# Pooled attention and a token/channel mixer on one core: the first batch's transposed u made by matmuls, and the fourth batch's loads gated on the second batch's transposed u

## The chip, the cores and the metric

The kernel runs on one core of a Trainium2 chip. The metric is device time in microseconds (us) of one launch. Three runs of the kernel before gave 288.86, 289.02 and 290.66 us; their median is 289.02. One further execution was profiled: it took 290.2 us, of which the profile's span covers 288.5.

## The reference

Eight batches of 576 positions, eight heads of 64 columns. Keys and values are averaged over groups of eight positions, so that each head attends over 72 pooled positions. The result x (576 x 512 per batch) goes through a mixer over positions (tokens) and one over columns (channels):

```python
k_p = k.reshape(B, H, Sp, pool, D).mean(axis=3)          # Sp = 72, pool = 8
v_p = v.reshape(B, H, Sp, pool, D).mean(axis=3)
attn = softmax(scale * np.matmul(q, k_p.transpose(0, 1, 3, 2)))
x = np.matmul(attn, v_p)  ->  (B, 576, 512)
xt = x.transpose(0, 2, 1)
h = np.maximum(xt @ w_tok1, 0.0) @ w_tok2                # 576 -> 256 -> 576 over positions
u = x + h.transpose(0, 2, 1)
h2 = np.maximum(u @ w_ch1, 0.0) @ w_ch2                  # 512 -> 1536 -> 512 over columns
out = u + h2
```

## The kernel before, in words

All operands of matmuls are bf16, sums are fp32 in PSUM; the loads cast from fp32. Batches are numbered 0 to 7, so the fourth batch of the title is batch 3 and the second is batch 1. A batch has 512 "main" positions in four blocks of 128 (j = 0 to 3) and a "tail" of 64; the tails of two batches share one tile of 128 rows. The pairs are (0, 7), (1, 2), (3, 4) and (5, 6).

A batch passes through these steps, by their names in the code:

- `pool_k` (L255 to L281): pools the keys by matmuls (L267, L271) and copies them into a block tile `kbd`, of which there are three. `pool_v` does it for the values of batches 0 and 1 on PE; from batch 2 on `sum_v` (L292) adds the values up on POOL, twelve instructions a batch.
- `do_qT` (PE) or `qT_dma` (a transposing DMA on SP, L540, from batch 2 on): the queries, transposed. Half of the positions are unit a (`jj` = 0), half unit c; the tail is unit t.
- `do_S` scores on PE, maximum and subtraction on DVE (L329, L331); `do_E` the exponential on ACT (L339); `do_PT` transposes the probabilities (PE and a copy on ACT or DVE for batches 0 and 1, L350 and L352; DMA on SP from batch 2 on, L346); `do_AV` weighs the values (L387, in batch 0 L375) and divides on DVE.
- `do_AT` / `do_both_AT`: first token matrix and Relu, into `AT`; `do_u`: second token matrix and the residual, into `um`; `do_uT`: u transposed into `uTm`, on PE for batch 0 (L530), by DMA from batch 1 on (L526).
- `channel_mix`: `do_GT` is the first channel matrix with Relu on ACT (L756, L758; L787 for the first three blocks of batch 0), `out_pieces` the second one (L771) with the residual u added on DVE (L775) and the store on SP (L803).

The order on every engine is written out by hand: lists of steps with a weight, which `weave` (L29) merges. While the channel mix of batch b runs, `second_stream` (for batch 1) or `value_stream` of batch b+1 and `score_stream` of batch b+2 are woven in. Each engine executes its instructions in that order, and one that waits holds up all that follow it on its engine. POOL issues all loads, in order, among its own additions; SP issues the transposing DMAs and the stores.

A load goes into a tile that an earlier batch has used: two sets for keys and queries, one for values (`vs`). The loads of batches 0, 1 and 2, and batch 3's keys and queries, are issued at once, as far as their tiles are free (L823 to L827, with `sum_v(2)` behind them); batch 3's values and its sums stand in `second_stream` (L670). From batch 4 on `load_gated` (L737) issues a batch's loads: a one-column copy on POOL that reads a given tile holds back all that follows on POOL, then come the loads, then `sum_v`. Batch 4's loads wait in this way for the last transposed probabilities of batch 2 (L726).

PSUM has six buffers of one bank for general use (`pa`) and two for transposes (`pt`).

Of the kernel before, what the change touches and what calls it, by code (L numbers as in the profile page):

```python
# [8 lines left out]
FP32 = mybir.dt.float32  # L9
# [39 lines left out]
def kernel(  # L49
# [10 lines left out]
):  # L60

# [240 lines left out]
    class Unit:  # L302
# [40 lines left out]
        def do_PT(self, e):  # L343
            self.pT[e] = pt_pool.tile([P, H, P], BF16, name="pT")
            if not self.by_pe:
                nc.sync.dma_start_transpose(out=self.pT[e], in_=self.probs[:, e].rearrange("p h n -> p (h n)"))  # L346
                return
            pT_ps = ps_tr.tile([SP, H, P], BF16, name="pt")
            for h in range(H):
                nc.tensor.transpose(out=pT_ps[:, h, :], in_=self.probs[:, e, h, 0:SP], identity=ident)  # L350
            by_dve = e == 0 and self.jj == 1 if self.first else e == 1
            (nc.vector.tensor_copy if by_dve else nc.scalar.copy)(out=self.pT[e][0:SP], in_=pT_ps)  # L352
# [106 lines left out]
    def token_mix(b):  # L459
# [26 lines left out]
        def do_both_AT(js, tail, last):  # L486

            fresh = not at_both
            if fresh:
                at_both.extend(ps.tile([P, DM], FP32, name="pa") for _ in range(2))  # L490
            for i, j in enumerate(js):
                for m in range(2):
                    nc.tensor.matmul(out=at_both[m], lhsT=w1m[:, j, m * P:(m + 1) * P], rhs=x_main[b][:, j, :],
                                     start=(fresh and i == 0), stop=(last and i == len(js) - 1))
            if tail:
                for m in range(2):
                    nc.tensor.matmul(out=at_both[m], lhsT=w1t[s][:, m * P:(m + 1) * P], rhs=x_tail[g],
                                     start=False, stop=False)
            if last:
                for m in range(2):  # L500
                    acts(m, at_both[m])

        def do_u(j):
            u_ps = ps.tile([P, DM], FP32, name="pa")
            by_act = b == 0 and j % 2 == 1
            if j < NJ:
                if by_act:
                    nc.tensor.matmul(out=u_ps, lhsT=ident, rhs=x_main[b][:, j, :], start=True, stop=False)
                for m in range(2):
                    nc.tensor.matmul(out=u_ps, lhsT=w2m[:, m, j, :], rhs=ATs[b][:, m, :],  # L510
                                     start=(m == 0 and not by_act), stop=(m == 1))
                if by_act:
                    nc.scalar.copy(out=u_main[b][:, j, :], in_=u_ps)
                else:
                    nc.vector.tensor_tensor(out=u_main[b][:, j, :], in0=u_ps, in1=x_main[b][:, j, :], op=ALU.add)  # L515
            else:
                for i in range(4):
                    nc.tensor.matmul(out=u_ps, lhsT=w2t[i // 2][:, i % 2, :], rhs=ATs[groups[g][i // 2]][:, i % 2, :],  # L518
                                     start=(i == 0), stop=(i == 3))
                nc.vector.tensor_tensor(out=u_tail[g], in0=u_ps, in1=x_tail[g], op=ALU.add)  # L520

        def do_uT(j):
            us = u_main[b][:, j, :] if j < NJ else u_tail[g]
            if b > 0:
                dst = uT_main[b][:, :, j * P:(j + 1) * P] if j < NJ else uT_tail[g]
                nc.sync.dma_start_transpose(out=dst, in_=us)  # L526
                return
            uT_ps = ps_tr.tile([P, 4, P], BF16, name="pt")
            for kk in range(4):
                nc.tensor.transpose(out=uT_ps[:, kk, :], in_=us[:, kk * P:(kk + 1) * P], identity=ident)  # L530
            copy = nc.scalar.copy if j % 2 else nc.vector.tensor_copy
            copy(out=uT_main[b][:, :, j * P:(j + 1) * P], in_=uT_ps)

        return do_AT, do_both_AT, do_u, do_uT
# [32 lines left out]
    def mix_stream(st, b, pooled=()):  # L567
# [3 lines left out]
        u_main[b] = u_pool.tile([P, NJ, DM], BF16, name="um")  # L571
# [4 lines left out]
        do_AT, do_both_AT, do_u, do_uT = token_mix(b)  # L576
        if b == 0:
            return do_both_AT, do_u, do_uT
# [5 lines left out]
        for j in range(nj + 1):  # L584
            if j < nj:
                add(690, do_u, j)
            if j >= 1:
                add(0 if b else 224, do_uT, j - 1)

    def first_stream():  # L590
# [5 lines left out]
        do_both_AT, do_u, do_uT = mix_stream(st, b)  # L596
# [20 lines left out]
        add(SC, t.do_S)  # L617
        add(PT, a.do_PT, 1)
        add(0, c.do_E, 2)
        add(AV, a.do_AV, 0)  # L620
        add(0, t.do_E)
        add(PT, c.do_PT, 0)
        add(AV, a.do_AV, 1)
        add(PT, c.do_PT, 1)
        add(PT, t.do_PT)
        add(1080, do_both_AT, (0, 1), False, False)
        add(AV, c.do_AV, 0)
        add(AV, t.do_AV)
        add(AV, c.do_AV, 1)
        add(1080, do_both_AT, (2,), True, False)  # L630
        add(540, do_both_AT, (3,), False, True)
        k1 = []
        add(690, do_u, 0)
        add(690, do_u, 1)
        add(224, do_uT, 0)
        add(690, do_u, 2)
        add(224, do_uT, 1)
        add(690, do_u, 3)
        add(KP, lambda: k1.append(pool_k_sum(1)))
        add(224, do_uT, 2)  # L640
        add(224, do_uT, 3)
        add(0, lambda: pool_k_copy(1, k1[0]))
        return st

    def second_stream(st):
# [7 lines left out]
        add(VP, pool_v, b)  # L653
        add(SC, a.do_S, 1)
# [9 lines left out]
        add(PT, a.do_PT, 1)  # L664
        add(SC, t.do_S)
        add(0, c.do_E, 1)
        add(AV, a.do_AV, 0)
        add(SC, c.do_S, 2)
        add(0, t.do_E)
        add(0, load, 3, (2,))  # L670
        add(0, sum_v, 3)
        add(AV, a.do_AV, 1)
        add(0, c.do_E, 2)
        add(PT, t.do_PT)
        add(PT, c.do_PT, 0)
        add(AV, t.do_AV)
        add(PT, c.do_PT, 1)
# [4 lines left out]
        mix_stream(st, b, owned(2))  # L682

# [59 lines left out]
    def channel_mix(uTs, us, dst, width, early=0):  # L743

        GT = gt_pool.tile([P, NM, width], BF16, name=f"GT{width}")
# [13 lines left out]
        def out_pieces(j, halves=1):  # L761
            n, w = NM // 3, DM // halves
            pieces = []
            for c in range(halves):
                cols, hold = slice(c * w, (c + 1) * w), {}

                def do_out(part, cols=cols, hold=hold):
                    if part == 0:
                        hold["ps"] = ps.tile([P, w], FP32, name="pa")
                    for kk in range(part * n, (part + 1) * n):  # L770
                        nc.tensor.matmul(out=hold["ps"], lhsT=GT[:, kk, j * P:(j + 1) * P], rhs=wc2[:, kk, cols],  # L771
                                         start=(kk == 0), stop=(kk == NM - 1))
                    if part == 2:
                        o_sb = out_pool.tile([P, w], FP32, name="o")
                        nc.vector.tensor_tensor(out=o_sb, in0=hold["ps"], in1=us(j)[:, cols], op=ALU.add)  # L775
                        dst(j, cols, o_sb)
# [5 lines left out]
        def do_early(m, hold, t0, t1):  # L782
            def f():
                if t0 == 0:
                    hold[m] = ps.tile([P, width], FP32, name="pa")
                for kk in range(4):
                    nc.tensor.matmul(out=hold[m][:, t0:t1], lhsT=wc1[:, kk, m * P:(m + 1) * P], rhs=uTs[:, kk, t0:t1],  # L787
                                     start=(kk == 0), stop=(kk == 3))
                if t1 == width:
# [4 lines left out]
        wide = [(432, do_early(m, hold, *t)) for t in ((0, width // 2), (width // 2, width)) for m in range(early)]  # L794
        return wide + [(864, do_GT(m0)) for m0 in range(early, NM, per)], out_pieces

    def c_stream(b):
# [11 lines left out]
        wide, chunk = channel_mix(uT_main[b], lambda j: u_main[b][:, j, :], dst_main, MAIN, 0 if b else 3)  # L809
# [15 lines left out]
    load(2)  # L825
    load(3, (0, 1))
    sum_v(2)  # L827
# [44 lines left out]
```

## Time and profile before

| | |
|---|---|
| three runs, us | 288.86, 289.02, 290.66 (median 289.02) |
| the profiled execution, us | 290.2, span 288.5 |
| busy, us (share of the span) | PE 271.0 (94%), DVE 162.4 (56%), ACT 121.3 (42%), POOL 101.5 (35%) |
| PE busy, 60 to 70 us and 70 to 80 us | 7.36 and 8.46 of 10 |
| granted PE clock, 70 to 80 us | 0.83 (1.00 in the other stretches of ten) |
| PE busy, 120 to 270 us | 148.9 of 150 |
| chain that ended last | PE 82%, DMA 7%, DVE 6%, ACT 3% |

Rows of the profile name a line of the kernel, an engine, an operation with its output and input tiles, and a count; times are us from the span's start, and a bracket holds the idle time ahead of the row and what ended it. PE's matmuls are pipelined: a row's duration runs to a modelled end, and what one matmul costs in a row of many is the distance between starts. "To landing" of a DMA counts from its issue.

### The profile page before, as it was taken

The page shows a single profiled execution, that of the slowest core. Times are in us where ns is not written, and L with a number is a line of the kernel's source. Part 1 is how long each engine was busy: PE and PEld are TensorE (multiplying, and loading weights), DVE is VectorE, ACT ScalarE, POOL GpSimd, SP SyncE. Part 2 cuts the span into 40 slices and gives each one's busy share as a digit, 9 for nine tenths or more (in the row PEclk, how much of TensorE's full clock was granted, in tenths as well). Part 3 has the DMA queues.
Part 4 walks back from the last instruction along what each step waited for, and adds up shares of the span by engine and source line. Part 5 has one row for each costly group of instructions (what it writes and reads, how often), then busy time and mean ns, then how long its engine had stood idle before and what let it go on. Part 6 is the DMA issues. An engine that isn't in the chain of part 4 may idle for free.

```text
span 288.5 us, 5632 instructions
## 1 busy us (share of the span) xinstructions
PE 271.0 (94%) x2210; PEld 147.1 (51%) x2246; DVE 162.4 (56%) x371; ACT 121.3 (42%) x222; POOL 101.5 (35%) x147
## 2 busy tenths in 40 slices
PE   6888998885999999999999999999999999999995
PEld 4554755442445554446545554465445444464463
DVE  4676268687356985386647953684558642530012
ACT  8572887113442355114553365035442561026320
POOL 8666634292780836129508423570000000000000
PEclk9999999999899999999999999999999999999999
DMA  7999999999959999998999799959524820241013
GB/s 84 185 205 198 196 204 192 174 203 146 252 88 169 166 214 195 182 183 166 172 185 155 170 218 153 157 165 162 115 54 97 194 58 36 93 109 39 27 45 110
DMA packets 102714, 42.68 MB, mean 148 GB/s; under 512 B 72480, under 2 KB 98080, under 8 KB 102688
## 3 DMA queue, kind: packets, MB, share of 16 engines
q0 software_dynamic: 36688, 17.93, 47.2%
q1 hardware_dynamic: 65856, 24.26, 43.7%
q8 instruction: 17, 0.28, 0.4%
q10 hardware_dynamic: 144, 0.13, 0.1%
q14 instruction: 9, 0.07, 0.1%
HBM read 35.85 MB, written 9.44 MB: 157 GB/s over the span
## 4 chain that ended last, share of the span: by engine, by line
PE 82%; DMA 7%; DVE 6%; ACT 3%; issue 1%; DVEq 0%
PE pa L756 31%; PE pa L771 28%; DMA qT<-qm 4%; PE pa L510 4%; PE pa L472 4%; PE pa L387 3%; DMA uTm<-um 3%; PE pa L253 2%; PE pa L326 2%; DVE sh L331 2%; DVE mx L329 1%; PE pa L267 1%; ACT prob_m L339 1%; PE pa L518 1%; ACT pT L352 1%
## 5 line engine op out<-in xcount | busy, mean ns | idle before, releaser
L771 PE MATMUL pa<-wc,GT 128*128 128x512 bf16 (+1 forms) x429 | 102.7, 373 | 1.0 <-DVE sh L331 0.2
L756 PE MATMUL pa<-uTm,wc 128*128 128x512 bf16 x357 | 90.1, 384 | 3.8 <-DMA uTm<-um 3.1
L758 ACT ACTIVATE GT<-pa 128x512 bf16<-128x512 f32 x105 | 62.5, 597 | 66.5 <-PE pa L756 62.4
L756 PEld LDWEIGHTS <-wc 128*128 128x128 bf16 x564 | 45.4, 98 | 40.6 <-DVE o L775 3.6
L771 PEld LDWEIGHTS <-GT 128*128 128x128 bf16 x444 | 41.5, 98 | 40.4
L339 ACT ACTIVATE prob_m<-sh 128x432 bf16<-128x432 f32 (+1 forms) x48 | 24.7, 522 | 60.9 <-DVE sh L331 51.1
L298 POOL TENSOR_TENSOR s<-vs 72x512 f32<-72x512 bf16 x24 | 27.6, 1148 | 49.7 <-DMA vs<-in_v_dram 48.2
L775 DVE TENSOR_TENSOR o<-pa,um 128x512 f32<-128x512 f32 (+1 forms) x33 | 22.1, 670 | 25.3 <-PE pa L771 25.3
L329 DVE TENSOR_REDUCE mx<-pa 128x6 f32<-128x432 f32 (+1 forms) x48 | 26.4, 550 | 7.6 <-PE pa L326 7.5
L331 DVE TENSOR_TENSOR sh<-pa,mx 128x432 f32<-128x432 f32 (+1 forms) x48 | 26.8, 558 | 5.1 <-DVE mx L329 0.5
L391 DVE RECIPROCAL den<-pa 128x4 f32<-128x4 f32 (+1 forms) x66 | 11.6, 176 | 24.5 <-PE pa L387 24.4
L515 DVE TENSOR_TENSOR um<-pa,xm 128x512 bf16<-128x512 f32 x30 | 20.2, 687 | 8.6 <-PE pa L510 8.6
L392 DVE TENSOR_TENSOR xm<-pa,den 128x256 bf16<-128x256 f32 x56 | 23.8, 424 | 1.9
L510 PE MATMUL pa<-AT,w2m 128*128 128x512 bf16 x64 | 18.3, 379 | 0.5 <-ACT AT L466 0.5
L299 POOL TENSOR_TENSOR s<-s 72x256 f32<-72x256 f32 x24 | 17.3, 722 | 1.9
L468 DVE TENSOR_SCALAR AT<-pa 128x512 bf16<-128x512 f32 x8 | 5.5, 692 | 21.8 <-PE pa L476 21.1
L387 PEld LDWEIGHTS <-pT 72*128 72x128 bf16 (+1 forms) x280 | 12.4, 100 | 8.8 <-issue 1.7
L326 PE MATMUL pa<-kbd,qT 128*128 128x144 bf16 x128 | 15.5, 226 | 1.4 <-DMA qT<-qm 0.9
L326 PEld LDWEIGHTS <-qT 128*128 128x128 bf16 x128 | 10.7, 98 | 10.5 <-DMA qT<-qm 1.4
L387 PE MATMUL pa<-vpx,pT 72*128 72x65 bf16 (+1 forms) x280 | 14.1, 194 | 1.1 <-DVE pT L352 0.5
L472 PE MATMUL pa<-xm,w1m 128*128 128x512 bf16 x54 | 14.4, 379 | 0.4 <-DVE xm L392 0.2
L253 PE MATMUL pa<-idle 128*128 128x288 bf16 (+2 forms) x40 | 9.8, 379 | 2.3 <-DVE pool_t L178 2.2
(122 smaller groups left out, 232.8 us busy)
## 6 DMA issues: line engine op xcount, KB each, us to landing
out_dram<-o SPq DMA_DIRECT2D x31, 256.0 KB, 2.6
km<-in_k_dram POOLq DMA_DIRECT2D x8, 512.0 KB, 7.7
qm<-in_q_dram POOLq DMA_DIRECT2D x7, 512.0 KB, 12.7
vs<-in_v_dram POOLq DMA_DIRECT2D x6, 576.0 KB, 10.1
wc<-in_moe_w_ch_dram POOLq DMA_DIRECT2D x6, 512.0 KB, 12.4
out_dram<-o SPq DMA_DIRECT2D x9, 128.0 KB, 2.4
vs<-in_v_dram POOLq DMA_DIRECT2D x2, 512.0 KB, 9.9
kt<-in_k_dram POOLq DMA_DIRECT2D x8, 64.0 KB, 7.7
```

Of the source, the lines that this page charges most:

```text
L298: nc.gpsimd.tensor_tensor(out=s4, in0=vs[:, hs, 0:4], in1=vs[:, hs, 4:8], op=add)
L326: nc.tensor.matmul(out=sc[:, (h - h0) * 2:(h - h0) * 2 + 2, :], lhsT=qTs[self.b][:, 2 * h + self.jj, :], rhs=kbd[self.b % NB][:, h], start ...
L329: nc.vector.tensor_reduce(out=mx[:, 0:n], in_=sc, axis=AX.X, op=ALU.max)
L331: nc.vector.tensor_tensor(out=sh[:, 0:n], in0=sc, in1=mx[:, 0:n, None].broadcast_to([P, n, SP]), op=ALU.subtract)
L339: nc.scalar.activation(out=self.probs[:, :, h0:h1, 0:SP].rearrange("p e h n -> p h e n"), in_=self.sh[i][:, 0:(h1 - h0) * 2].rearrange("p ...
L387: nc.tensor.matmul(out=ao[r, hh, :], lhsT=probs_of(h, r), rhs=vpx[b % NB][:, h, :], start=True, stop=True)
L392: nc.vector.tensor_tensor(out=xo[rows, hf * HP * D:(hf + 1) * HP * D].rearrange("p (h d) -> p h d", d=D), in0=ao[rows, :, 0:D], in1=den[ro ...
L472: nc.tensor.matmul(out=at_ps, lhsT=w1m[:, j, m * P:(m + 1) * P], rhs=x_main[b][:, j, :], start=(j == 0), stop=False)
L510: nc.tensor.matmul(out=u_ps, lhsT=w2m[:, m, j, :], rhs=ATs[b][:, m, :], start=(m == 0 and not by_act), stop=(m == 1))
L756: nc.tensor.matmul(out=g_ps[:, i, :], lhsT=wc1[:, kk, m * P:(m + 1) * P], rhs=uTs[:, kk, :], start=(kk == 0), stop=(kk == 3))
L758: nc.scalar.activation(out=GT[:, m0:m0 + per, :], in_=g_ps, func=AF.Relu)
L771: nc.tensor.matmul(out=hold["ps"], lhsT=GT[:, kk, j * P:(j + 1) * P], rhs=wc2[:, kk, cols], start=(kk == 0), stop=(kk == NM - 1))
```

## The change

Batch 0's steps are put in another order, and u is no longer made as such for its main positions. Instead the four PSUM banks that hold uT are started with x transposed (matmuls of x against the identity, `do_xT`), between the token-mixing matmuls, and the second token matrix is then added with its operands exchanged, so that u comes out transposed (`do_uT0`); four copies write `uTm`. Since batch 0 has no `um` any longer, its residual is added in the second channel matrix by four matmuls of `uTm` against the identity per block, and DVE copies the sum. The tail's token matmul becomes the last one. Unit c's second transposed probabilities go through a `pa` buffer. The pooling of batch 1's keys goes behind all of that, and the first three blocks of batch 0's channel mix are split by the contracted index instead of by columns.

Batch 1's steps are reordered too; its unit c's second copy goes from DVE to ACT. Batch 2's queries are loaded ahead of its keys, its values from `second_stream`. All of batch 3's loads are taken out of their places and issued by `load_gated`, behind the last of batch 1's four transposes of u.

```diff
 def do_PT(self, e):
-            pT_ps = ps_tr.tile([SP, H, P], BF16, name="pt")
+            if self.first and self.jj and e:
+                pT_ps = ps.tile([SP, H, P], BF16, name="pa")
+            else:
+                pT_ps = ps_tr.tile([SP, H, P], BF16, name="pt")
...
-            by_dve = e == 0 and self.jj == 1 if self.first else e == 1
+            by_dve = e == 0 and self.jj == 1 if self.first else e == 1 and self.jj == 0
 # token_mix
+        uT_ps = []
+        def do_xT(js):
+            if not uT_ps:
+                uT_ps.extend(ps.tile([P, MAIN], FP32, name="pa") for _ in range(4))
+            for j in js:
+                for kk in range(4):
+                    nc.tensor.matmul(out=uT_ps[kk][:, j * P:(j + 1) * P], lhsT=x_main[b][:, j, kk * P:(kk + 1) * P],
+                                     rhs=ident, start=(j == 0), stop=False)
+        def do_uT0():
+            for m in range(2):
+                for kk in range(4):
+                    nc.tensor.matmul(out=uT_ps[kk], lhsT=ATs[b][:, m, kk * P:(kk + 1) * P],
+                                     rhs=w2m[:, m].rearrange("p j n -> p (j n)"), start=False, stop=(m == 1))
+            for kk in range(4):
+                (nc.vector.tensor_copy if kk % 2 else nc.scalar.copy)(out=uT_main[b][:, kk, :], in_=uT_ps[kk])
 # first_stream
+        add(0, c.do_E, 2)
         add(PT, a.do_PT, 1)
-        add(0, c.do_E, 2)
         add(AV, a.do_AV, 0)
         add(0, t.do_E)
         add(PT, c.do_PT, 0)
+        add(PT, c.do_PT, 1)
         add(AV, a.do_AV, 1)
-        add(PT, c.do_PT, 1)
+        add(AV, c.do_AV, 0)
         add(PT, t.do_PT)
+        add(AV, c.do_AV, 1)
         add(1080, do_both_AT, (0, 1), False, False)
-        add(AV, c.do_AV, 0)
         add(AV, t.do_AV)
-        add(AV, c.do_AV, 1)
-        add(1080, do_both_AT, (2,), True, False)
-        add(540, do_both_AT, (3,), False, True)
-        k1 = []
...
+        add(0, do_xT, (0, 1))
+        add(540, do_both_AT, (2,), False, False)
+        add(0, do_xT, (2,))
+        add(540, do_both_AT, (3,), False, False)
+        add(0, do_xT, (3,))
+        add(540, do_both_AT, (), True, True)
+        add(690, do_uT0)
+        add(KP, pool_k, 1)
 # second_stream
         add(VP, pool_v, b)
+        add(0, load, 2, (2,))
+        add(0, sum_v, 2)
...
-        add(0, load, 3, (2,))
-        add(0, sum_v, 3)
...
         mix_stream(st, b, owned(2))
+        add(0, load_gated, 3, lambda: uT_main[b][:, 3, MAIN - 1:MAIN])
 # channel_mix, out_pieces
+                        if us is None:
+                            for kk in range(4):
+                                nc.tensor.matmul(out=hold["ps"][:, kk * P:(kk + 1) * P], lhsT=uTs[:, kk, j * P:(j + 1) * P],
+                                                 rhs=ident, start=False, stop=(kk == 3))
+                            nc.vector.tensor_copy(out=o_sb, in_=hold["ps"])
+                        else:
+                            nc.vector.tensor_tensor(out=o_sb, in0=hold["ps"], in1=us(j)[:, cols], op=ALU.add)
 # channel_mix, do_early
-                for kk in range(4):
-                    nc.tensor.matmul(out=hold[m][:, t0:t1], lhsT=wc1[:, kk, m * P:(m + 1) * P], rhs=uTs[:, kk, t0:t1],
+                for kk in range(k0, k0 + 2):
+                    nc.tensor.matmul(out=hold[m], lhsT=wc1[:, kk, m * P:(m + 1) * P], rhs=uTs[:, kk, :],
                                      start=(kk == 0), stop=(kk == 3))
 # the loads ahead of the streams
     load_w_ch2()
-    load(2)
-    load(3, (0, 1))
-    sum_v(2)
+    load(2, (1, 0))
```

## The prediction

> **What bounds the kernel now.** I read the page's busy shares and 40 slices first, then the chain that ended last, the list of waits, and the order of time on PE, POOL and SP. PE is busy 94% of the span, and in the chain PE has 82% and DMA 7%. So the time is PE's work plus the few places where PE stands. In PE's order of time the largest one lies between the first and the second batch's channel mix:
>
> ```profile
> 61.65 0.36 PE L326 MATMUL pa<-kbd,qT 128*128 128x144 bf16 x3 [0.94 <-DMA qT<-qm]
> ...
> 71.49 5.24 PE L756 MATMUL pa<-uTm,wc 128*128 128x512 bf16 x16 [3.13 <-DMA uTm<-um]
> 76.57 0.42 PE L387 MATMUL pa<-vpx,pT 72*128 72x65 bf16 x8
> ...
> 94.51 0.69 PE L267 MATMUL pa<-pool_m,km 128*64 128x64 bf16 x32
> ```
>
> The bracket is idle time ahead of the row and its cause. Twice PE waits for a transposing DMA: 0.94 us for batch 2's qT, 3.13 us for batch 1's uT. After the second wait, 16 matmuls take 71.49 to 76.57 = 5.08 us, against 16 x 0.216 = 3.45 (four such take 0.86 in the chain): 1.63 us lost, with a granted clock of 0.85, 0.50 and 0.80 in the 2 us windows from 70, 72 and 74. Keep the last row in mind: from 94.51, where batch 4's keys are pooled, to the end PE runs for 288.5 - 94.51 = 194.0 us with hardly a gap.
>
> The chain shows why the two transposes are late:
>
> ```profile
> 49.10 12.50 DMA qT<-qm
> ...
> 64.03 7.32 DMA uTm<-um
> ```
>
> They fly while POOL's loads of batches 2 and 3 fill the same DMA engines (191 to 198 GB/s from 44 to 54 us). From 180 us on, with hardly a load left, the median uTm transpose lands in 2.5 us.
>
> The loads hang on POOL, which issues them in order, between its own sums:
>
> ```profile
> 65.06 0.86 POOL L131 DMA_DIRECT2D vs<-in_v_dram  x1
> ...
> 73.14 1.15 POOL L298 TENSOR_TENSOR s<-vs 72x512 f32<-72x512 bf16 x1 [6.73 <-DMA vs<-in_v_dram]
> ...
> 83.24 0.19 POOL L739 COPY gate<-pT 128x1 bf16<-128x1 bf16 x1
> 83.36 0.92 POOL L138 DMA_DIRECT2D km<-in_k_dram  x1
> ...
> 110.81 0.92 POOL L138 DMA_DIRECT2D km<-in_k_dram  x1 [0.31 <-PE pa L756]
> ...
> 115.30 0.87 POOL L131 DMA_DIRECT2D vs<-in_v_dram  x1
> ...
> 127.74 1.15 POOL L298 TENSOR_TENSOR s<-vs 72x512 f32<-72x512 bf16 x1 [11.58 <-DMA vs<-in_v_dram]
> ```
>
> Batch 3's values are issued at 65.06, land 7.9 us later, and are summed in 10.1 us (73.14 to 83.24). The gate for batch 4 has no idle ahead of it: POOL itself is the limit there, and batch 4's keys, issued at 83.36, land at 89.6 (6.2 us), only 4.9 us before PE pools them at 94.51.
>
> **Part 1, the first batch's new order.** It drops two identity matmuls of 512 columns (0.43 us), four adds and casts of u and four copies of uT. 16 matmuls of 128 columns replace 16 transposes of that size; both orders have eight u matmuls. PE's path: the last token-mixing matmul ends near 26.1 (before: 25.6), since the first xT needs four banks and so waits about 1.1 us for the tail's DVE multiply; the Relus take it to 26.6, eight u matmuls to 28.4. Then comes batch 1's key pooling, whose keys land at 19.54 + 8.7 = 28.2, so it ends near 29.1 while the four copies of uT finish at 29.5. The early matmuls start at 29.1 instead of 30.45 and need 12 x 0.216 = 2.6, against 24 starts over 2.8: the next row is reached at 31.7 instead of 33.28. Gain 1.5 us; bounds 0 (other buffers late) and 2.5.
>
> Batch 0's residual moves to PE: 4 x 4 matmuls of 128 columns at 0.055 us (eight such take 0.45 from start to start) = +0.9. DVE's copy replaces an add of the same 128x512 f32 (0.67 us): nothing.
>
> **Part 2, the second batch's order.** PE's small waits there are 0.39, 0.76, 0.52 and 0.25 = 1.9 us, each on an ACT or DVE step just ahead. The order puts more matmuls between; c's second copy moves from DVE (0.69) to ACT (1.01), behind the tail's values and four output matmuls. I take half, 1.0 (bounds 0 and 1.9). Batch 2's queries go out ahead of its keys, and batch 3's keys and queries leave the queue altogether, so the 0.94 for qT goes too.
>
> **Part 3, the gated loads, first their gain.** Without loads in flight uT's transposes should land in 2.5 us; bounds 2.5 and 7.3. The last was issued at 64.03; with 1.5 + 1.0 us gained and 0.2 given to one identity group ahead of it, 61.7, landing at 64.2. PE would reach it at about 68.4 - 3.4 + 0.9 = 65.9, so the 3.13 wait and the 1.63 of slow clock both go. Sum so far at 94.51: 1.5 + 1.0 + 0.9 + 3.1 + 1.6 - 0.9 = 7.3 us (rounded rows); PE is ready to pool batch 4's keys at 87.2.
>
> **Part 3, the price.** POOL's queue is now: batch 2's sums (its values land some 3 us earlier, so they end near 63), the gate on uT, then keys, two key tails, queries, two query tails and values of batch 3, batch 3's sums, and only then the gate and keys of batch 4. Behind the new gate, therefore, stands all that batch 4 needs. Before, batch 3's keys and queries went out from 36.00 on, and only the values were left for after 65. Term by term:
>
> - uT lands: 64.2
> - gate and first issue, as 110.31 to 110.81: 64.7
> - to the values' issue, as 110.81 to 115.30 (4.49): 69.2
> - values land, as 115.30 plus 12.3 (the one other bundle of the same make-up, batch 5's): 81.5. Bounds: 7.9, values alone at 65.06, and 12.3
> - sums, 10.1: 91.6
> - keys issued at 91.8, landed by 6.2 (bounds 6.0 and 7.7): 98.0
>
> PE, ready at 87.2, stands at the key pooling until 98.0: a wait of 10.8 us. The clock afterwards costs 1.6 again, by the row at 71.49 (bounds 0 and 3). From there to the end nothing changes: 194.0 us, and batch 4's later needs keep their distance (values needed a stage later; the gate of batch 5 idled 6.16 us before). Span: 98.0 + 194.0 + 1.6 = 293.6, that is -7.3 + 10.8 + 1.6 = **+5.1 us** on 288.5. The profiled execution itself took 290.2 (span plus 1.7 around it), which would become 295.3; the three runs' median is 289.0, so I forecast 294.1.
>
> No row here shows PE idle for 11 us. [...]
>
> **The rivals.**
>
> *Loads at full rate (not slower).* The bundle is 1.90 MB as landed. With nothing else to share, at the 195 GB/s of the first 45 us and 2 us from issue to first bytes (83.36 to about 85.4), values would land at 64.7 + 2.0 + 9.7 = 76.4 and keys at 76.4 + 10.1 + 0.2 + 2.0 + 2.7 = 91.4: span 91.4 + 194.0 + 1.6 = 287.0, time 287.5, -0.5%. Against it: batch 5's bundle took 128 to 130 GB/s, and here five pT transposes and two 256 KB stores fall into the same stretch. It decides when the values land within 7 us of issue. [...]
>
> *The loads don't bind (faster).* If batch 4's keys were there by 87.2, only the 7.3 us would show: 281.7. Every term from the gate on would have to shrink by 11 us together; 10.1 us of sums alone speak against it.
>
> *The first batch gains nothing (slower still).* If the new order only trades waits, the last transpose goes at 64.0 and lands at 67.5 at the latest that I think likely; every us moves the end by a us: 297.4.
>
> *The change does not do what it says.* If uT's transposes stay at 7.3 us without loads, the keys come 4.8 us later still: 298.9. The 2.5 us median speaks against it.
>
> **How the numbers follow.** About 1% (2.9 us) is what a measurement of this kernel can tell from no change, so "same" is 286.1 to 291.9. Forecast, with values landing in 10 to 12.3 us: 0.60, 292 to 297. Full rate or between: 0.20, 286.1 to 292. Loads don't bind, or full rate with a further gain: 0.10, below 286.1. The two later cases: 0.10, 297 to 300. That gives faster 0.10, same 0.20, slower 0.70. The range leaves out the fastest case and the far end of the late ones: 287.0 to 298.5.
>
> **What would show it.** The waits should list PE (weight load or matmul) L267-equivalent, pooling keys, behind km by 6 to 12 us near 87 to 98; the 3.1 us behind uTm and the 0.9 behind qT should be gone; the last uTm should land in under 4 us; POOL's sums of batch 3 should start near 81 and its next gate come near 92. The forecast is wrong if the values land within 7 us, if PE reaches the pooling later than 92 for a reason that I missed, or if uT lands after 67.

## The result, and the profile after

The changed kernel is slower: 305.3 us (304.98 to 306.3, four runs) against 289.84 us for the kernel before in the same series; the ratio is 1.053, with a 95% interval of 1.046 to 1.060. The profiled execution took 306.3 us with a span of 304.6, which is 16.1 us more than the 288.5 of before. The forecast was 294.1, the range 287.0 to 298.5: the sign was right, the size was not, and the time lies above the range.

First PE of the changed kernel in order of time, the rows that answer to those shown of before:

```profile
58.47 0.35 PE L327 MATMUL pa<-kbd,qT 128*128 128x144 bf16 x3
...
65.44 3.62 PE L763 MATMUL pa<-uTm,wc 128*128 128x512 bf16 x16
...
72.60 0.46 PE L391 MATMUL pa<-vpx,pT 72*128 72x65 bf16 x8 [2.41 <-DMA pT<-prob_m]
...
77.01 0.65 PE L391 MATMUL pa<-vpx,pT 72*64 72x65 bf16 x8 [2.25 <-DMA pT<-prob_t]
...
80.76 0.62 PE L391 MATMUL pa<-vpx,pT 72*128 72x65 bf16 x8 [1.28 <-DMA pT<-prob_m]
...
87.35 0.62 PE L391 MATMUL pa<-vpx,pT 72*128 72x65 bf16 x8 [4.26 <-DMA pT<-prob_m]
...
108.65 1.06 PE L268 MATMUL pa<-pool_m,km 128*64 128x64 bf16 x32 [5.09 <-DMA km<-in_k_dram]
```

The first two rows have lost their brackets: the waits of 0.94 us for qT and of 3.13 us for uTm are gone, batch 2's first scores start 3.2 us earlier than before (58.47 against 61.65) and batch 1's channel mix 6.05 us earlier (65.44 against 71.49). The 16 matmuls now take 3.46 us to the next row at 68.90, at a granted clock of 1.00. Then come five brackets that were not there before. Four of them, 10.2 us in all, are waits for batch 2's transposed probabilities, pT, and one of 5.09 us is for batch 4's keys. Those are pooled at 108.65; before, at 94.51.

The chain that ended last, through the same stretch (start, duration, what):

```profile
62.83 2.46 DMA uTm<-um
65.34 0.19 POOL gate L745
...
70.07 19.22 DMA vs<-in_v_dram
...
99.64 8.97 DMA km<-in_k_dram
```

uT is quick now: 2.46 us instead of 7.32. The two long pieces are batch 3's values and batch 4's keys. POOL's order of time shows how they hang together:

```profile
65.34 0.19 POOL L745 COPY gate<-uTm 128x1 bf16<-128x1 bf16 x1 [1.78 <-DMA uTm<-um]
65.59 0.92 POOL L139 DMA_DIRECT2D km<-in_k_dram  x1
...
70.07 0.87 POOL L132 DMA_DIRECT2D vs<-in_v_dram  x1
89.43 1.14 POOL L299 TENSOR_TENSOR s<-vs 72x512 f32<-72x512 bf16 x1 [18.49 <-DMA vs<-in_v_dram]
...
99.52 0.19 POOL L745 COPY gate<-pT 128x1 bf16<-128x1 bf16 x1
99.64 0.93 POOL L139 DMA_DIRECT2D km<-in_k_dram  x1
```

The gate opens at 65.34, the values are issued at 70.07 and can be read at 89.43, 19.4 us later; the sums take 10.1 us; the next gate opens without idle time at 99.52, and batch 4's keys land 9.0 us after their issue at 99.64. The granted clock falls too. This is the line of granted clock in the page's 40 slices of 7.6 us:

```profile
PEclk9999999997558959999999999999999999999999
```

Four slices, from 68.5 to 99 us, are low, and one from 106.6 to 114.2, behind the wait for the keys. In the first stretch, with the four waits of 1.3 to 4.3 us between 70 and 88, it is 0.50 in each window of 2 us from 74 to 92.

A view that the prediction does not use is the busy share of the 16 DMA engines in the same stretch, 30 to 110 us in 40 slices of 2 us (tenths, 9 is 90% or more). Before:

```profile
DMA  9999999999999999998999999503999999999969
```

and after:

```profile
DMA  9999999999999045368999999999994000269999
```

Before, the DMA engines are busy through these 80 us, but for three slices from 80 to 86, around the end of POOL's sums, and a dip from 106 to 108. After, they have two holes: from 56 to 66, while POOL sums batch 2's values and then stands at its gate, with no load of batch 3 issued yet, and from 90 to 100, while POOL sums batch 3's values. What isn't moved in the first hole is moved in the next 20 us, where the transposes of pT are also due. The experiments take this apart.

### The profile page after: what moved, and what is told of

Read it like the earlier page. It is cut to its first block, busy times and chain, and to the rows that moved or that the text cites. A ratio compares the mean times of both kernels' runs of the same rounds, so it can differ in the third digit from the quotient of the medians.

```text
span 304.6 us, 5671 instructions
## 1 busy us (share of the span) xinstructions
PE 281.0 (92%) x2248; PEld 148.8 (49%) x2248; DVE 161.2 (53%) x368; ACT 120.7 (40%) x221; POOL 101.7 (33%) x148
## 2 busy tenths in 40 slices
DMA packets 102714, 42.68 MB, mean 140 GB/s; under 512 B 72480, under 2 KB 98080, under 8 KB 102688
## 3 DMA queue, kind: packets, MB, share of 16 engines
q0 software_dynamic: 36688, 17.93, 46.6%
q1 hardware_dynamic: 65856, 24.26, 42.1%
## 4 chain that ended last, share of the span: by engine, by line
PE 78%; DMA 10%; POOL 5%; DVE 4%; issue 1%; ACT 1%; DVEq 0%; POOLq 0%
PE pa L778 28%; PE pa L763 27%; DMA vs<-in_v_dram 6%; PE pa L510 3%; PE pa L476 3%; DMA km<-in_k_dram 3%; PE pa L254 3%; PE pa L391 2%; PE pa L327 2%; PE pa L268 2%; POOL s L299 2%; DVE sh L332 1%; DVE mx L330 1%; PE pt L354 1%; POOL s L300 1%; PE pa L800 1%
## 5 line engine op out<-in xcount | busy, mean ns | idle before, releaser
L778 PE MATMUL pa<-wc,GT 128*128 128x512 bf16 (+1 forms) x444 | 105.9, 378 | 0.0
L763 PE MATMUL pa<-uTm,wc 128*128 128x512 bf16 x372 | 94.2, 392 | 0.0
L299 POOL TENSOR_TENSOR s<-vs 72x512 f32<-72x512 bf16 x24 | 27.6, 1148 | 76.5 <-DMA vs<-in_v_dram 75.1
L788 DVE TENSOR_TENSOR o<-pa,um 128x512 f32<-128x512 f32 (+1 forms) x29 | 19.4, 669 | 25.9 <-PE pa L778 25.9
L396 DVE TENSOR_TENSOR xm<-pa,den 128x256 bf16<-128x256 f32 x56 | 23.8, 424 | 1.9
L391 PE MATMUL pa<-vpx,pT 72*128 72x65 bf16 (+1 forms) x280 | 14.7, 199 | 10.2 <-DMA pT<-prob_m 8.0
L512 DVE TENSOR_TENSOR um<-pa,xm 128x512 bf16<-128x512 f32 x28 | 18.8, 687 | 8.2 <-PE pa L510 8.2
L391 PEld LDWEIGHTS <-pT 72*128 72x128 bf16 (+1 forms) x280 | 12.7, 103 | 20.3 <-DMA pT<-prob_m 10.3
L510 PE MATMUL pa<-AT,w2m 128*128 128x512 bf16 x56 | 15.8, 379 | 0.0
L476 PE MATMUL pa<-xm,w1m 128*128 128x512 bf16 x56 | 15.4, 398 | 0.1
L254 PE MATMUL pa<-idle 128*128 128x288 bf16 (+2 forms) x42 | 11.1, 402 | 2.2 <-DVE pool_t L179 2.2
```

Of the source, the lines that this page charges most:

```text
L299: nc.gpsimd.tensor_tensor(out=s4, in0=vs[:, hs, 0:4], in1=vs[:, hs, 4:8], op=add)
L391: nc.tensor.matmul(out=ao[r, hh, :], lhsT=probs_of(h, r), rhs=vpx[b % NB][:, h, :], start=True, stop=True)
L396: nc.vector.tensor_tensor(out=xo[rows, hf * HP * D:(hf + 1) * HP * D].rearrange("p (h d) -> p h d", d=D), in0=ao[rows, :, 0:D], in1=den[ro ...
L476: nc.tensor.matmul(out=at_ps, lhsT=w1m[:, j, m * P:(m + 1) * P], rhs=x_main[b][:, j, :], start=(j == 0), stop=False)
L763: nc.tensor.matmul(out=g_ps[:, i, :], lhsT=wc1[:, kk, m * P:(m + 1) * P], rhs=uTs[:, kk, :], start=(kk == 0), stop=(kk == 3))
```

## The experiments

All times are against runs of the kernel before in the same series (medians 289.8 to 291.3 us). Theory S says that the loss comes from the gated loads alone. Rival P says that the new orders cost a part of it. Rival O says that the gated bundle takes 19 us by its own size, whatever flies beside it. Each experiment's number stands in this table with the moment at which PE pools batch 4's keys, and what is left from there to the end of the span (before: 94.51 and 194.0 us). These last two columns are of the one profiled execution, which is not always near the median: e11's took 293.5 us, e2's 308.7 and e5's 305.9, the others' within 1.0 of it.

| kernel | us (lowest to highest) | ratio, 95% | keys pooled | rest |
|---|---|---|---|---|
| the changed kernel | 305.3 (305.0 to 306.3) | 1.053 (1.046 to 1.060) | 108.65 | 196.0 |
| e2, only the loads | 307.0 (306.9 to 308.7) | 1.058 (1.054 to 1.062) | 110.90 | 196.1 |
| e5, keys and queries as before | 304.4 (303.7 to 305.9) | 1.047 (1.044 to 1.050) | 108.57 | 195.4 |
| e6, values first | 303.0 (302.5 to 304.0) | 1.043 (1.039 to 1.048) | 106.98 | 194.2 |
| e3, gate behind pT | 302.2 (301.1 to 303.3) | 1.040 (1.036 to 1.045) | 104.83 | 195.1 |
| e4, batch 4's keys first | 299.6 (298.5 to 300.7) | 1.031 (1.027 to 1.035) | 102.86 | 194.5 |
| e8, e3 and e4 together | 299.6 (298.9 to 301.1) | 1.032 (1.027 to 1.036) | 100.40 | 197.0 |
| e9, as e7 with the old orders | 298.4 (297.2 to 299.1) | 1.026 (1.022 to 1.031) | 91.40 | 205.6 |
| e7, bundle split over two gaps | 297.7 (296.8 to 301.2) | 1.026 (1.021 to 1.031) | 93.79 | 201.3 |
| e11, orders, values alone gated | 296.0 (293.5 to 296.4) | 1.017 (1.013 to 1.020) | 96.44 | 195.4 |
| e10, first batch's order alone | 294.6 (292.8 to 295.4) | 1.011 (1.007 to 1.014) | 99.12 | 194.2 |
| e12, before, values alone gated | 294.3 (293.5 to 295.6) | 1.011 (1.008 to 1.015) | 95.93 | 196.6 |
| e1, only the orders | 293.7 (292.5 to 295.1) | 1.011 (1.008 to 1.014) | 97.89 | 193.9 |

### e1 and e2: the two halves of the change

e1 has both new orders with the loads as they were before:

```diff
-    load(2, (1, 0))
+    load(2)
+    load(3, (0, 1))
+    sum_v(2)
 # second_stream
-        add(0, load, 2, (2,))
-        add(0, sum_v, 2)
...
+        add(0, load, 3, (2,))
+        add(0, sum_v, 3)
         add(AV, a.do_AV, 0)
...
-        add(0, load_gated, 3, lambda: uT_main[b][:, 3, MAIN - 1:MAIN])
```

e2 is the reverse: the kernel before with the changed kernel's loads.

> The changed kernel's two orders of work, with the loads as they were before the change. Theory S (the loss comes from the gated loads alone: they share the DMA engines with batch 2's transposes, and batch 4's keys queue behind them on POOL): faster than before, 286 to 288.5 us, since PE reaches batch 1's u 2.3 us earlier (55.65 against 57.96) and the rest of the trace stays as before. Rival P (the new orders cost part of the loss): 291 us or more.

> The orders of work as before the change, with only the loads changed (batch 2's queries first, all of batch 3's loads behind batch 1's last transpose of u). Theory S: 304 to 308 us, the whole loss and about 2 us more than the full change, because the gate opens about 2 us later. Rival P: clearly less than the full change's 305, below 300.

e2 came out as S said: 307.0 us, so the loads alone cost all that the change costs. Its gate opens at 69.39, its values land in 18.4 us (issue 74.12, sums from 92.52), and PE waits 7.63 us for batch 4's keys (PE of e2):

```profile
110.90 1.07 PE L267 MATMUL pa<-pool_m,km 128*64 128x64 bf16 x32 [7.63 <-DMA km<-in_k_dram]
```

About 2 us of these late moments belong to this execution and not to the edit: the row that starts at 25.09 in the kernel before starts at 27.28 here, ahead of the first changed load (31.58); the three other executions took 306.9 to 307.0 us. e1 speaks against S: the orders alone don't gain 2 to 4 us, they lose 1.1%, as P has it. PE of e1 in order of time:

```profile
61.72 0.54 PE L327 MATMUL pa<-kbd,qT 128*128 128x144 bf16 x3 [3.18 <-DMA qT<-qm]
...
74.81 5.30 PE L762 MATMUL pa<-uTm,wc 128*128 128x512 bf16 x16 [4.47 <-DMA uTm<-um]
```

PE arrives earlier at both transposes, but qT lands no earlier (61.7 in both kernels) and uT 3.3 us later (74.8 against 71.5), so the two waits of before (0.94 and 3.13) grow to 3.18 and 4.47. With these loads, what the orders gain on PE is lost again at the transposes.

### e3, e4, e6: where the gated bundle's 19 us come from

e3 leaves everything as in the changed kernel and opens the gate for batch 3's loads later, behind batch 2's last pT:

```diff
 # second_stream
-        add(0, load_gated, 3, lambda: uT_main[b][:, 3, MAIN - 1:MAIN])
 # score_stream, at its end
+        if b == 2:
+            add(0, load_gated, 3, lambda: c.pT[1][:, 0, 0:1])
```

e4 puts batch 4's gate, keys and queries ahead of batch 3's sums:

```diff
 # load_gated
         nc.gpsimd.tensor_copy(out=gate, in_=ready())
+        if b == 3:
+            load(b, (0, 1, 2))
+            return
+        if b == 4:
+            load(b, (0, 1))
+            sum_v(3)
+            load(b, (2,))
+        else:
+            load(b, (0, 2, 1) if slot_of[b] else (0, 1, 2))
-        load(b, (0, 2, 1) if slot_of[b] else (0, 1, 2))
         sum_v(b)
```

e6 issues batch 3's values ahead of its keys and queries:

```diff
-        load(b, (0, 2, 1) if slot_of[b] else (0, 1, 2))
+        load(b, (2, 0, 1) if b == 3 else (0, 2, 1) if slot_of[b] else (0, 1, 2))
```

> The changed kernel, but the gate ahead of batch 3's loads waits for batch 2's last transposed probabilities instead of batch 1's transposed u, so that the loads no longer fly beside those transposes. Theory S: PE's 10.2 us of waits for pT shrink to under 3, the gate opens near 75, the values land 11 to 13 us after their issue instead of 19.4, and the time is about that of the change, 302 to 307. Rival O (the bundle takes 19 us by its own size): values 19 us after issue, 310 us or more.

> The changed kernel, but POOL issues batch 4's gate, keys and queries ahead of batch 3's sums; batch 4's values stay behind those sums. If POOL's order is what makes batch 4's keys late, PE's wait for km (5.1 us) goes, and with it the slow clock after it: 298 to 300.5 us. If the keys are late for another reason: 304 us or more.

> The changed kernel, but batch 3's values go first in the gated bundle, ahead of its keys and queries. The values then land 10 to 13 us after the gate instead of 24, the sums end near 88, and batch 4's keys, held by the gate on the last transposed probabilities, are issued near 88 and land near 97, before PE asks for them: the 5.1 us wait goes, the 10 us of waits for transposed probabilities stay: 297 to 301 us. If the waits for transposed probabilities are what counts alone: no change, 304 or more.

e3 decides between S and O. The same bundle with no pT beside it, POOL in order of time:

```profile
78.17 0.87 POOL L132 DMA_DIRECT2D vs<-in_v_dram  x1
88.50 1.14 POOL L299 TENSOR_TENSOR s<-vs 72x512 f32<-72x512 bf16 x1 [9.46 <-DMA vs<-in_v_dram]
```

The values are there 10.3 us after their issue, not 19.4: O falls. What e3 takes away from the bundle are the five pT and two stores; a transpose of the queries (qT) flies beside the end of both. Stores alone don't make the difference: batch 5's bundle in the kernel before had two beside it and landed in 12.3 us. The other side is as clear, in SP's own row (SPq is SP's queue; the second number is the time that the pair of issues took). In the changed kernel:

```profile
70.11 6.69 SPq L347 DMA_TRANSPOSE pT<-prob_m  x2
```

and in e3:

```profile
68.95 2.64 SPq L347 DMA_TRANSPOSE pT<-prob_m  x2
```

From issue to landing, batch 2's transposes of probabilities took 2.7 to 3.4 us in e3, 3.2 to 15.0 (median 9.0) in the changed kernel. So, side by side, the load took about twice its time, and the transposes' median went up to nearly three times. The page of the changed kernel counts the packets of both on the same 16 DMA engines: POOL's loads (17.93 MB) take 46.6% of their time, the queue with SP's transposes and stores (24.26 MB) 42.1%.

Yet e3 gains only 3.1 us. PE no longer waits for pT, but it has run ahead of the keys, and stands where the forecast had put the wait (PE of e3):

```profile
104.83 1.06 PE L268 MATMUL pa<-pool_m,km 128*64 128x64 bf16 x32 [12.44 <-DMA km<-in_k_dram]
```

It also waits 0.98 and 1.14 us for batch 3's keys and 2.27 for its qT, since those loads are late now. The keys of batch 4 are issued late, but land fast (POOL of e3):

```profile
98.70 0.93 POOL L139 DMA_DIRECT2D km<-in_k_dram  x1
```

From 98.70 to 104.83 are 6.1 us, against 9.0 in the changed kernel. There batch 2's uT are issued beside these keys, from 98.33 on; in e3 they and the tail's uT are issued by 96.7, ahead of the keys.

e4 takes the keys out from behind the sums, and they wait for nobody (PE of e4):

```profile
86.73 0.62 PE L391 MATMUL pa<-vpx,pT 72*128 72x65 bf16 x8 [3.22 <-DMA pT<-prob_m]
...
102.86 0.69 PE L268 MATMUL pa<-pool_m,km 128*64 128x64 bf16 x32
```

The time is 299.6 us, as expected, 5.7 less than the changed kernel, whose wait for these keys was 5.09. But PE still reaches the pooling at 102.86, because the four waits for pT (2.71, 2.81, 1.30 and 3.22 us) and the slow clock stay (four matmuls take 1.68 us from 87.17 on; in the changed kernel 16 took 3.46 from 65.44 on). So the changed kernel has two limits, 5 us apart: the keys behind the sums (108.65), and the transposes beside the loads (PE ready at 103.56).

e6 meets its expectation halfway. The values land in 10.2 us and batch 4's keys are issued 14 us earlier, at 85.67, which ends their wait; but that puts batch 4's loads beside batch 3's qT, which PE now awaits for 6.17 us (PE of e6):

```profile
104.45 0.54 PE L327 MATMUL pa<-kbd,qT 128*128 128x144 bf16 x3 [6.17 <-DMA qT<-qm]
```

The time is 303.0 instead of 297 to 301.

### e7, e8, e9: can the bundle be put elsewhere?

e8 is e3 and e4 together. e7 splits the bundle: batch 3's keys and queries go out early, behind batch 2's values, and batch 3's values with batch 4's keys and queries behind batch 2's pT. e9 is e7 with the old orders.

```diff
 # e7, second_stream
         add(0, load, 2, (2,))
+        add(0, load, 3, (0, 1))
         add(0, sum_v, 2)
...
-        add(0, load_gated, 3, lambda: uT_main[b][:, 3, MAIN - 1:MAIN])
 # score_stream, at its end, as in e3; load_gated
+        if b == 3:
+            nc.gpsimd.tensor_copy(out=gate, in_=ready())
+            load(3, (2,))          # e8: load(3, (0, 1, 2))
+            load(4, (0, 1))
+            sum_v(3)
+            return
+        if b == 4:
+            load(4, (2,))
+            sum_v(4)
+            return
```

> The changed kernel's orders, with batch 3's loads split: keys and queries behind batch 2's values, before any transpose of u; behind batch 2's last transposed probabilities come batch 3's values and batch 4's keys and queries, then batch 3's sums, then batch 4's values. If the loss comes only from loads that share the DMA engines with SP's transposes and from POOL's order, no wait of PE on a DMA above 1 us is left between 60 and 110 us, and the time is 282 to 286, the 7.3 us of gain that was forecast. If the waits on uT or qT stay because batch 3's queries still fly: 287 to 291.

> All of batch 3's loads and then batch 4's keys and queries behind batch 2's last transposed probabilities, batch 3's sums after them. Against the late gate alone (302.2 us) PE's 12.4 us wait for batch 4's keys should shrink to under 2, the 2.3 us for batch 3's qT and the 2.1 us for its keys stay: 288 to 291 us. If POOL's order is not what makes those keys late: 300 or more.

> The orders of work as before the change, with the split loads. If the new orders are worth what the hand count said (1.5 us in batch 0, 1.0 in batch 1, less 0.9 for the identity matmuls), this is about 1.6 us slower than the split loads with the new orders, and 3 to 5 us faster than before: 284.5 to 287. If the orders are worth nothing, the same as those.

None of the three expectations holds. e7 pools batch 4's keys without a wait and even 0.7 us earlier than the kernel before, and e9 3.1 us earlier; but the rest, 194.0 us in the kernel before, grows to 201.3 and 205.6. Up to the pooling e7 still waits 2.22 us for qT and 2.95 for uT, the case that its expectation put at 287 to 291; whether batch 3's queries are the cause no run tells. What neither case had are two waits behind the pooling, PE of e7:

```profile
107.69 0.43 PE L391 MATMUL pa<-vpx,pT 72*128 72x65 bf16 x8 [3.05 <-DMA pT<-prob_m]
...
116.12 0.23 PE L391 MATMUL pa<-vpx,pT 72*64 72x65 bf16 x3 [2.27 <-POOL vpx L301]
```

The first is batch 3's pT, which now flies beside batch 4's values (issued at 96.86); the second is the shared tail of batches 3 and 4, which needs batch 4's sums as well, and those end at 116.0. Together they are 5.3 of the 7.3 us that the rest grew by, and the granted clock is 0.50 from 108 to 110. e9 differs from e7 by 0.7 us, and their ranges overlap, so with these loads too the new orders are worth nothing that can be measured. In e8 it is batch 3's qT that meets the loads (PE of e8):

```profile
97.86 0.54 PE L327 MATMUL pa<-kbd,qT 128*128 128x144 bf16 x3 [9.82 <-DMA qT<-qm]
```

Each placement that frees one wait meets another: uT in the kernel before, pT in the changed kernel, batch 4's keys in e3, qT in e8, and pT of the next batch in e7.

### e5, e10, e11, e12: values alone behind the gate, and the first order alone

e5 puts batch 3's keys and queries back into the early queue and gates only its values. e10 has batch 0's new order alone; batch 1's order and all loads are as before. e11 is e1, and e12 the kernel before, each with one edit: batch 3's values, and nothing else, behind the gate on uT.

```diff
 # e5, against the changed kernel
     load(2, (1, 0))
+    load(3, (0, 1))
 # e5, e11, e12: load_gated
-        load(b, (0, 2, 1) if slot_of[b] else (0, 1, 2))
+        if b == 3:
+            load(b, (2,))
+        else:
+            load(b, (0, 2, 1) if slot_of[b] else (0, 1, 2))
 # e11, e12: second_stream, against e1 and the kernel before
-        add(0, load, 3, (2,))
-        add(0, sum_v, 3)
...
         mix_stream(st, b, owned(2))
+        add(0, load_gated, 3, lambda: uT_main[b][:, 3, MAIN - 1:MAIN])
```

> After's orders; batch 3's keys and queries go back to their old place in the queue (issued ahead of batch 2's values, as far as their buffers are free), and only batch 3's values stay behind the gate on batch 1's last uT. If the loss is the size of the gated bundle: uT's wait is gone, the gate opens at 65, the values are issued at 65 to 66 and land in 8 to 9 us (74), the sums end at 84, batch 4's keys are issued at 84 and land at 90.5; PE pools them there and the time is 90.5 + 194 + 1.7 = 286 to 289, the old time or a little better. If POOL's chain is only pushed elsewhere (batch 2's values, issued later than before, end their sums after 65, or batch 2's transposes still meet loads): 290 to 296, with the wait for vpx, qT or pT to be seen on PE.

> Batch 0's new order with u made transposed by matmuls, alone: batch 1's order and all loads as before. By the rows so far it gains 0.8 us by the next row after the early matmuls and gives 0.9 us back for 16 identity matmuls, and the loads keep the rest in place: 288.5 to 291, no difference. If the 1.1% that both orders lost with the old loads came from batch 0's order: 292.5 to 294.5.

> After's orders, all loads in the place they had before, and only batch 3's values moved: from the middle of batch 1's steps to behind the gate on batch 1's last uT. With both orders and without this gate the values were issued at 62.9, met the transposes of u and landed in 12 us. If it is this meeting that eats the gain of the orders: the last uT lands near 65, the values are issued there and land in 8 us (73), the sums end at 83, batch 4's keys land at 89 to 90, PE's wait for uT is under 2 us, and the time is 284 to 289. If batch 3's values stay late by more than the gate saves (landing in 10 us or more beside the transposes of batch 2's probabilities): sums end after 86, keys land after 92.5, 289 to 293.

> The kernel before with batch 3's values alone behind the gate on batch 1's last uT, all orders and other loads as before. Before, the values were issued at 65.06, when three of the four transposes of u were already out, and PE waited 3.1 us for them. If the meeting on the DMA engines is what costs: uT lands near 68.5 instead of 71.4, PE's wait is about 1 us or less, the values are issued near 69 and land at 77, sums to 87, keys to 93.5 against PE's arrival at 91 to 92: 287 to 290, about no change. If uT is late for another reason (its wait stays above 2.5 us): the values come 6 us later on top, and the time is 292 to 296.

e5, at 304.4 us, lies beyond both of its cases. Batch 2's values now stand in the queue behind batch 3's keys and queries. POOL of e5:

```profile
49.40 0.85 POOL L132 DMA_DIRECT2D vs<-in_v_dram  x1 [2.04 <-PE pa L391]
74.14 1.15 POOL L299 TENSOR_TENSOR s<-vs 72x512 f32<-72x512 bf16 x1 [23.89 <-DMA vs<-in_v_dram]
```

They land 24.7 us after their issue, so the sums, the gate (84.23) and batch 4's keys (issued 101.53) are late as a chain, and uT beside those loads costs PE 7.71 us.

e10 answers what e1 had left open: batch 0's order alone loses the 1.1% that both orders lose, so batch 1's order adds nothing measurable. On PE that order does in e10 what it does in the changed kernel: the row after the early matmuls is reached at 32.56 (32.51 there, 33.28 before). What changes is POOL's order. In the code batch 2's values stand ahead of batch 3's keys in both kernels, but these early loads are not issued in the order of the code, and the two change places:

```profile
38.14 0.85 POOL L132 DMA_DIRECT2D vs<-in_v_dram  x1 [1.81 <-PE pa L290]
38.98 0.90 POOL L139 DMA_DIRECT2D km<-in_k_dram  x1
...
52.16 1.15 POOL L299 TENSOR_TENSOR s<-vs 72x512 f32<-72x512 bf16 x1 [1.75 <-DMA vs<-in_v_dram]
...
61.75 0.86 POOL L132 DMA_DIRECT2D vs<-in_v_dram  x1
```

Before, batch 3's keys went out ahead of batch 2's values (36.00 and 38.81); here they go behind. Batch 2's sums start 3.3 us earlier (before: 55.50), and so batch 3's values go out 3.3 us earlier (before: 65.06): right beside the last three transposes of u, issued from 61.13 on. The last of those lands near 75.1 instead of 71.4, and PE waits 4.01 us for it, after 2.02 for qT; behind the first the granted clock falls to 0.50 (64 to 66 us), and behind the second 16 matmuls take 5.99 us (75.19 to 81.18) instead of the 3.46 of the changed kernel. Why the new order of batch 0 turns the two loads round was not tried.

e11 shows that this meeting is real. With the values held back, the last uT lands at 69.1 instead of 74.8 in e1, and of PE's wait of 4.47 us 0.82 is left, but PE waits for a later transpose in its place (PE of e11):

```profile
69.19 3.61 PE L764 MATMUL pa<-uTm,wc 128*128 128x512 bf16 x16 [0.82 <-DVE sh L332]
...
78.19 0.65 PE L391 MATMUL pa<-vpx,pT 72*64 72x65 bf16 x8 [3.13 <-DMA pT<-prob_t]
```

e11 lies above both of its ranges (296.0 us, in a profile of its fastest execution 293.5): the values land in 8.9 us, but they are issued at 69.35 and not at 65. e12 does the same to the kernel before: of its 3.13 us for uT 1.23 are left, and 3.29 us for the tail's pT come (PE of e12):

```profile
69.57 3.61 PE L758 MATMUL pa<-uTm,wc 128*128 128x512 bf16 x16 [1.23 <-DVE sh L331]
...
78.72 0.45 PE L387 MATMUL pa<-vpx,pT 72*64 72x65 bf16 x8 [3.29 <-DMA pT<-prob_t]
```

The bracket puts the 1.23 us down to DVE, but uT landed at 69.5 too, so a faster DVE would hardly have shortened them. e12's first expectation (no change) is missed by about 1%: PE pools batch 4's keys at 95.93 without a wait for them, but 1.4 us later than before, and the rest grows by 2.6 us with waits for batch 2's uT (1.30) and batch 3's pT (0.98). The last uT lands at 69.5 even with no load of values beside it. In e11 and e12 the DMA engines are busy until 66 to 67 all the same, without that load. So of the last uT's 7.3 us in the kernel before, batch 3's values cause about two (landed at 71.4 against 69.5). From 55 to 80 us of e12, the packets of the queue with SP's transposes and stores take 90.5% of the DMA engines' time and those of POOL's loads 43.7% (batch 3's values, issued at 69.72, among them), some of it at once. The rest of uT's time goes only when batch 3's keys and queries are held back too, as in the changed kernel and e2; which part of it is theirs and which that of the other transposes was not tried.

None of the twelve kernels beats the kernel before.

## Why the prediction was wrong, step by step

*Part 1.* The gain at the row after the early matmuls was put at 1.5 us (bounds 0 and 2.5); it is 33.28 - 32.51 = 0.77. Batch 1's keys are pooled from 29.18, not from 28.4, so the early matmuls start at 29.91 instead of 29.1. The identity matmuls cost what they should: 0.22 us for four (65.22 to 65.44), 0.9 in all, so that on PE the first batch gains nothing on balance. What I had not priced is that the order of POOL's issues changes with it; with the old loads that costs 1.1% (e10).

*Part 2.* Right: batch 1's u starts at 55.65 against 57.96, of which 0.8 us is part 1's and 1.5 this part's (forecast: 1.0, bounds 0 and 1.9), and the wait for qT is gone.

*Part 3, the gain.* Right: uT lands 2.46 us after its issue, its wait and the slow clock behind it are gone, and PE starts batch 1's channel mix at 65.44 (forecast: 65.9). Up to here the forecast holds within 0.5 us for PE. The gate opens later than thought, with the first load issued at 65.59 instead of 64.7, because the last uT is issued at 62.83 and not at 61.7.

*Part 3, the price.* The mechanism was the forecast one (gate, bundle, sums, gate, keys, one after the other on POOL), and two terms of the sum were mis-sized:

| term | forecast | measured |
|---|---|---|
| first issue behind the gate | 64.7 | 65.59 |
| from there to the values' issue | 4.5 | 4.48 |
| values: issue to sums | 12.3 | 19.36 |
| sums, and to the keys' issue | 10.3 | 10.21 |
| keys: issue to PE | 6.2 | 9.01 |
| keys pooled at | 98.0 | 108.65 |
| from there to the end | 195.6 | 195.95 |

The values' landing fails first. I took 12.3 us, the row of batch 5's bundle, and called it the upper bound; but beside that bundle SP had issued only two stores and one uT (121.02 to 124.90 in the kernel before) and, in its last 2.5 us, two more uT; beside this one there were five pT, two stores and from 81.41 on a qT. I named those five transposes as an argument against a faster landing, and did not let them lengthen the slower one. It is 7.1 of the 11.0 us that the span was missed by. The keys' landing, 2.8 us, is the same mistake: bounds of 6.0 and 7.7, where uT's transposes of batch 2 were issued from 98.33 on (e3, without them, has 6.1). The gate gives 0.9, the rest 0.3.

*What the forecast left out altogether* is that the transposes pay for the meeting as well. "PE, ready at 87.2" was 103.56 in fact; that PE might reach the pooling later than 92 for a reason that was missed is one of the signs of being wrong that the prediction names. From 65.44 the kernel before's steps would have brought PE there at 65.4 + 3.5 + 17.9 = 86.8; 10.2 us of waits for pT and 6.5 us of slow clock lie between. For the end this was nearly hidden, since the late keys cover it: e4, where the keys are on time, still takes 299.6 us, and by that alone the forecast would have been too low.

*"Batch 4's later needs keep their distance, values needed a stage later"* was wrong in its reason: the shared tail of batches 3 and 4 needs batch 4's values during batch 3 (2.27 us in e7). In the changed kernel it cost nothing, as the rest of 195.95 shows.

*The clock.* One gap costs what was said (1.6, bounds 0 and 3): the rest grows by 1.95 us after 5.09 idle, and in e3 by 1.1 us after 12.44, so here the longer gap did not cost more. The granted clock was 0.50 from 108 to 112 in the changed kernel and from 104 to 108 in e3, and 1.00 again from 114 and from 110. Several gaps in a row are another case: with the four waits for pT it was 0.50 for some 18 us (74 to 92).

*The rivals.* Loads at full rate fell: the values took 19.4 us, not under 7. "The loads don't bind" fell: PE waited 5.09 us for batch 4's keys. "The first batch gains nothing" was half true: on balance PE gains nothing there (0.77 less 0.9), but the last uT still went out at 62.83 and not at 64.0, and both are small beside the landing times. "The change does not do what it says" fell: uT's transposes were indeed slowed by loads, and are quick without them (2.46 us).

## What to carry to other kernels

The gate that kept loads away from uT saved no bytes (42.68 MB in both profiles); it left the DMA engines a hole (56 to 66 us), and batch 3's loads went out from 65.59 to 70.07, beside the transposes of pT, which then landed in 9.0 us (median; 3.2 in e3). So read the DMA engines' busy slices first: where they are busy from end to end, ask what the moved bytes will meet. In this kernel each placement that removed one wait met another. A 9 doesn't tell the rate, though: in the kernel before, slices shown as 9 between 30 and 110 us moved from 143 to 308 GB/s. Whether fewer bytes, rather than other places for them, would shorten these waits was not tried. And take the landing time of a load from a stretch with the same company, transposes above all, or widen its bound: here the same load took 10.3 and 19.4 us.

## What the runs showed of the hardware

- The same 1.9 MB bundle, cast on its way, took 14.8 us from the gate's first issue to the values with one transpose (qT, from 83.77 on) beside its end (e3: 73.69 to 88.50) and 23.8 us with five more and two stores (the changed kernel: 65.59 to 89.43). The last pair of batch 2's pT went from 2.64 to 6.69 us of SP's time.
- The granted clock fell to 0.50 after idle times of PE of 2.41 us (the changed kernel, at 72.60: 0.50 from 74 on) and 2.02 us (e10, at 62.45: 0.50 from 64 to 66). It stayed at 1.00 after 2.14 (e9, at 70.00: up to 76) and 2.22 us (e7, at 60.88: up to 66), and right after 2.71 us (e4, at 73.30; there it fell in the next gap, 0.91 from 74 to 76). So in these runs the length of one gap alone did not decide it; what did, no run shows.
- The same load of batch 2's values landed 16.7 us after its issue in the kernel before, 14.0 in e10 (issued ahead of batch 3's keys), 15.3 in the changed kernel (no load of batch 3 near it) and 24.7 in e5 (behind batch 3's keys and queries): in these four runs "issue to landing" is no property of the load. It was longer with batch 3's keys issued ahead of it (16.7 and 24.7), and not with them behind it (14.0, against 15.3 with none near).
